# Routing one-hots written for eight of 32 rows, a later sum of the result, and 35 instead of 33 steps of y per phase

## The chip, the cores and the metric

The kernel runs on one core of one Trainium2 chip. The metric is the time of one execution on the device in microseconds (us); the median of three runs stands for a kernel. The profile is one more execution, recorded by the hardware profiler. Its engines are PE (TensorE, matmuls), PEld (its weight loads), DVE (VectorE), ACT (ScalarE), POOL (GpSimd) and SP (SyncE, which here only issues DMAs).

## The reference, cut to what matters

Attention (4 batches, 8 heads, 576 positions) gives 2304 tokens of 512 numbers, a dense layer pair makes `x` of them (2304 x 512), and a routed layer follows. Only the end of the dense pair (`y = g @ w_out`) and the routing are touched here:

```python
cap = N // E                      # 2304 // 8 = 288
logits = x @ w_gate
flat = logits.flatten()
order = np.argsort(-flat)
assigned = -np.ones(N); counts = np.zeros(E)
for idx in order:
    tok, e = idx // E, idx % E
    if assigned[tok] >= 0 or counts[e] >= cap:
        continue
    assigned[tok] = e
    counts[e] += 1
for e in range(E):
    mask = assigned == e
    out[mask] = np.maximum(x[mask] @ w1[e], 0.0) @ w2[e]
```

## The kernel before, in words

The kernel runs in stages: attention, the first dense product (`mlp_in`), then the second dense product y together with the routing, then the eight experts. This change lies in the stage of y and routing, from 592.7 to 846.3 us of the profiled span.

**y.** `MlpOut.run` (L1027) is a generator. It computes y for 18 tiles of 128 tokens, in 16 steps each, 288 steps in all. A step is three matmuls of 128x512 (L1038). After every fourth step `parts` has ACT copy the high parts of four blocks for the next tile, and POOL subtract them from the source to get the low parts (helper `split`, L497 and L502, one instruction of 128x512 on each). So POOL gets one such instruction for every four steps. When tile 16 is done, `ready` is set; `first.gather` then has POOL fetch the rows of the first expert's tokens from DRAM, while PE computes tile 17.

**Routing.** `routing` (L750) is a generator too. The greedy loop of the reference is done in seven phases; in each, one expert fills up. All 2304 tokens lie as 128 partitions x 18 columns (T = 18), with eight experts beside (NE = 8). In one phase:

- `best` (L795) finds for each token its best expert among those still open: a one-hot `bst`, and its key in two halves, `khi` and `klo`. Its last instruction, in `above` (L824), makes `G`, the comparison of the key with 40 thresholds (128x720, bf16).
- `oh` (L843) is `bst` times `U`, the tokens that are still free (128x144). `ohb` (L845) is its cast to bf16 in sixteen copies (128x2304), so that a count comes out on all 128 rows.
- Six rounds follow, three for each half of the key. A round is a `count` (L831): 18 small matmuls with the columns of `ohb` as weights and those of `G` as data. DVE reads the count (`sat`, L861), moves it across rows (`tq`, L863; `tb`, L868) and makes the next `G`.
- A last count (L889) with `GE` picks the expert that fills up. Then come `star`, `lim`, a prefix sum by two small matmuls (L911, L912), `best` of the next phase, and `U`.
- `final` (L834) adds the tokens that got a place to `FIN`: `ao` (L836) and the sum (L837). It stands behind the first count of the next phase.

**What sets the order.** All instructions are issued in the order in which the program is written, and each engine works through its own list in that order. In `build`, the loop `for t in routing(...)` takes a number from each `yield` of routing and issues that many steps of y before it goes on. The numbers are in the tuple YS:

```python
YS = (2, 9, 3, 4, 5, 4, 18, 3)
```

So on PE a phase is: 9 steps of y, first count, 3 steps, count, 3 steps, count, 4 steps, count, 3 steps, count, 3 steps, count, 3 steps, the count with `GE`, 5 steps, the prefix sum. That is 33 steps. PE can do y while DVE works on the routing, and it stands still where the steps in between are done before DVE is. Behind the seventh phase come 4 steps, the prefix sum over `FB` (L945), 18 steps, and the product that gives the permutation (L976); what is left of y follows.

Of the kernel before, what the change touches and what calls it, by code (L numbers as in the profile page):

```python
# [12 lines left out]
BF = mybir.dt.bfloat16  # L13
I32 = mybir.dt.int32
AF = mybir.ActivationFunctionType
OP = mybir.AluOpType
# [8 lines left out]
NE = 8  # L25
# [715 lines left out]
def bc(ap, axis, n):  # L741

    ap = ap.unsqueeze(axis)
    shape = list(ap.shape)
    shape[axis] = n
    return ap.to_broadcast(shape)
# [7 lines left out]
def routing(net, cst, pools, lg, perm, first, spare):  # L754
# [3 lines left out]
    tc, nc, io = net.tc, net.nc, net.io  # L758
    V = nc.vector
    rp, rw, rps = pools  # L760
    T = NTT

    def small(shape, name, dt=F32, **kw):
        return rw.tile(shape, dt, name=name, **kw)

    yield YS[0]
    L = rp.tile([128, T, NE], F32, name="L")
# [10 lines left out]
    U = rp.tile([128, T], F32, name="U")  # L778
    V.memset(U, 1.0)
    FIN = rp.tile([128, T, NE], F32, name="FIN")  # L780
# [5 lines left out]
    V.memset(remc, float(CAP))  # L786
    zs = rp.tile([128, T + 1], F32, name="zs")
    V.memset(zs[:, 0:1], 0.0)
    zero = rp.tile([128, 1], F32, name="zero")
    V.memset(zero, 0.0)  # L790
    wr = cst["eix"][:, 1]
# [30 lines left out]
    def above(key, base, rnd):  # L822
        G = small([128, T, 40], "G", BF)
        V.scalar_tensor_tensor(G, bc(key, 2, 40), base, bc(cst["thr"][:, rnd], 1, T),  # L824
                               op0=OP.subtract, op1=OP.is_ge)
        return G

    def count(G, ohb, n):
        cnt = rps.tile([128, n], F32, name="rps")
        for t in range(T):  # L830
            nc.tensor.matmul(cnt, ohb[:, t].rearrange("p a e -> p (a e)"), G[:, t], start=t == 0, stop=t == T - 1)  # L831
        return cnt

    def final(oh, A):  # L834
        ao = small([128, T, NE], "ao")
        V.tensor_tensor(out=ao, in0=oh, in1=bc(A, 2, NE), op=OP.mult)  # L836
        V.tensor_tensor(out=FIN, in0=FIN, in1=ao, op=OP.add)  # L837

    bst, khi, klo, G = best()
    last = None  # L840
    for ph in range(NE - 1):
        oh = small([128, T, NE], "oh", bufs=2)
        V.tensor_tensor(out=oh, in0=bst, in1=bc(U, 2, NE), op=OP.mult)  # L843
        ohb = small([128, T, 16, NE], "ohb", BF)
        V.tensor_copy(ohb, bc(oh, 2, 16))  # L845
        yield YS[1]

        key = khi
        for half in range(2):
            base = zero  # L850
            low = zero
            for rnd in range(3):
                cnt = count(G, ohb, 40)
                if rnd == half == 0 and last is not None:
                    final(*last)
                if rnd == 1:
                    low = small([128, 1], "low")
                    V.tensor_scalar(low, mx, 41.0, None, op0=OP.mult)
                sat = small([128, 40], "sat")
                num = small([128, 1], "num")  # L860
                V.tensor_scalar(sat, cnt, remc, 0.0, op0=OP.is_ge, op1=OP.add, accum_out=num)  # L861
                tq = small([128, 32], "tq")
                V.transpose(tq, num.to_broadcast([128, 32]))  # L863

                tb = small([128, 32], "tb")
                old = (zero, low, base)[rnd]
                base = small([128, 1], f"base{half}{rnd}")
                V.tensor_tensor_reduce(out=tb, in0=tq, in1=old.to_broadcast([128, 32]), op0=OP.add, op1=OP.max,  # L868
                                       scale=(1681.0, 41.0, 1.0)[rnd], scalar=0.0, accum_out=base)
                if rnd < 2:  # L870
                    G = above(key, base, rnd + 1)
                elif half == 0:
                    k2 = small([128, T], "k2")
                    V.tensor_scalar(k2, khi, base, 65536.0, op0=OP.subtract, op1=OP.mult)
                    V.tensor_tensor(out=k2, in0=k2, in1=klo, op=OP.add)
                    key = k2
                    G = above(key, zero, 0)
                else:
                    GE = small([128, 2, T], "GE", BF)
                    V.tensor_scalar(GE[:, 0], key, base, None, op0=OP.is_gt)  # L880
                    V.tensor_scalar(GE[:, 1], key, base, None, op0=OP.is_equal)
                if rnd == 0:
                    mx = small([128, 1], "mx")
                    V.tensor_reduce(out=mx, in_=tq, axis=mybir.AxisListType.X, op=OP.max)
                yield YS[2] if rnd < 2 else YS[3] if half == 0 else YS[7]

# [21 lines left out]
        V.tensor_copy(Zb, Z)  # L908
        yield YS[4]
        zp = rps.tile([128, 2, T], F32, name="rps")  # L910
# [12 lines left out]
        if ph < NE - 2:  # L923
            bst, khi, klo, G = best()
# [4 lines left out]
        A = small([128, T], "A")  # L929
        V.tensor_tensor(out=A, in0=GE[:, 0], in1=sel, op=OP.add)  # L930

        V.scalar_tensor_tensor(U, A, 0.0, U, op0=OP.is_equal, op1=OP.mult)
        last = oh, A
    final(*last)

    op = small([128, NE], "op")
    V.tensor_scalar(op, lim, 0.0, None, op0=OP.is_gt)
    V.tensor_copy(oh, bc(U, 2, NE))
    V.tensor_tensor(out=oh, in0=oh, in1=bc(op, 1, T), op=OP.mult)
    V.tensor_tensor(out=FIN, in0=FIN, in1=oh, op=OP.add)  # L940
    FB = small([128, T, NE], "FB", BF)
    V.tensor_copy(FB, FIN)
    yield YS[5]
    ps = rps.tile([128, 2, T, NE], F32, name="rps")
# [20 lines left out]
    V.tensor_tensor(out=ohk, in0=ge[:, :, 0:24], in1=ge[:, :, 1:25], op=OP.subtract)  # L965
    V.tensor_scalar(kx, kx, -96.0, 96.0, op0=OP.mult, op1=OP.add)
    V.tensor_tensor(out=kx, in0=kx, in1=slot, op=OP.add)
    ohq = small([128, T, 16, NE], "ohb", BF).rearrange("p t a e -> p t (a e)")[:, :, 0:96]
    V.tensor_tensor(out=ohq, in0=bc(kx, 2, 96), in1=bc(cst["q96"], 1, T), op=OP.is_equal)
    dig = small([128, T, 2, 24], "dig", BF)  # L970
    for d in range(2):
        V.tensor_tensor(out=dig[:, :, d], in0=ohk, in1=bc(cst["ids"][:, d], 2, 24), op=OP.mult)
    yield YS[6]
    ps = rps.tile([96, 2, 24], F32, name="rps")
# [13 lines left out]

YS = (2, 9, 3, 4, 5, 4, 18, 3)


class MlpOut:
# [369 lines left out]
```

## Time and profile before

| what | value |
|---|---|
| median of 3 runs | 1085.62 us (1083.53 to 1089.73) |
| the profiled execution | 1086.05 us, of which the span from the first to the last instruction is 1084.3 us |
| busy share of the span | PE 95%, PEld 74%, DVE 65%, ACT 44%, POOL 31% |
| granted TensorE clock, mean | 0.986 of full speed |
| chain that ended last, by engine | PE 60%, issue 18%, DVE 14%, POOL 4%, DMA 2%, ACT 1% |
| in it, lines of the routing | `rps` L831 2%, `G` L824 2%, `ohb` L845 1% |

The chain that ended last is followed back from the last instruction: at each step to what released it. A row of the timeline gives the start, the duration, the engine, the line, what is written and read, how often, and in brackets the idle time of the engine before it and what ended it. A matmul's row lasts longer than the time until the next one can start, since matmuls are pipelined.

### The profile page before, as it was taken

What the parts mean: (1) busy time and instruction counts of PE and PEld (TensorE: products, weight loads), DVE (VectorE), ACT (ScalarE), POOL (GpSimd) and SP (SyncE); (2) the same over time, 40 slices, a digit from 0 to 9 for tenths busy, and PEclk for the clock granted to TensorE, in tenths of its full rate; (3) what the DMA queues carried; (4) which work ended last, traced back from release to release, by engine and by line L of the source; (5) the groups of instructions that cost most, each with busy time, mean ns of one, the idle gap of its engine ahead of it and who ended that gap; (6) DMA issues with size and microseconds to landing.
All of it is one profiled execution on the core that took longest, in us unless ns stands there. A gap on an engine that the chain in (4) does not pass through costs nothing.

```text
span 1084.3 us, 20220 instructions
## 1 busy us (share of the span) xinstructions
PE 1029.3 (95%) x7815; PEld 804.1 (74%) x7815; DVE 700.6 (65%) x1734; ACT 480.3 (44%) x1034; POOL 336.4 (31%) x360
## 2 busy tenths in 40 slices
PE   8599999999999999999999899899999999999996
PEld 5255776666665777787776677677778899999996
DVE  7699566656667298864346788778874555555551
ACT  5477676766666232332225121121223455555552
POOL 1122333334334044322116444333434222222111
PEclk8899999999999999999999999999999999999998
DMA  5733332121200355643410262222212676555300
GB/s 131 178 95 98 102 94 69 35 70 34 86 1 2 89 204 191 214 146 127 148 57 6 64 233 79 78 71 87 64 56 89 221 255 199 200 194 194 112 24 22
DMA packets 75748, 119.76 MB, mean 110 GB/s; under 512 B 10340, under 2 KB 38272, under 8 KB 74116
## 3 DMA queue, kind: packets, MB, share of 16 engines
q1 hardware_dynamic: 70156, 104.81, 30.5%
q0 software_dynamic: 3136, 9.46, 2.8%
q10 hardware_dynamic: 2360, 4.20, 1.1%
q8 instruction: 61, 1.00, 0.4%
q14 instruction: 35, 0.29, 0.1%
HBM read 84.24 MB, written 23.60 MB: 99 GB/s over the span
## 4 chain that ended last, share of the span: by engine, by line
PE 60%; issue 18%; DVE 14%; POOL 4%; DMA 2%; ACT 1%; SPq 0%; POOLq 0%; DVEq 0%; ACTq 0%
PE hps L595 17%; PE yps L1038 10%; PE tr L289 8%; PE sc L232 8%; PE av L316 7%; PE sc L149 4%; POOL ye L1155 2%; POOL out_dram L1195 2%; PE rps L831 2%; DVE gall L134 2%; DVE G L824 2%; PE lacc L670 1%; DMA xh<-gall 1%; DVE P L244 1%; DVE ohb L845 1%
## 5 line engine op out<-in xcount | busy, mean ns | idle before, releaser
L261 POOL TENSOR_SCALAR P<-P,r 128x576 f32<-128x576 f32 x144 | 108.2, 763 | 234.9 <-DVE r L259 175.6
L595 PE MATMUL hps<-xh 128*128 128x512 f32 (+1 forms) x640 | 149.9, 376 | 1.2 <-DVE xh L502 1.2
L252 ACT ACTIVATE P<-P,nm 128x576 f32<-128x576 f32 x144 | 111.1, 772 | 64.0 <-DVE nm L244 61.3
L595 PEld LDWEIGHTS hps<-xh 128*128 128x128 f32 x640 | 110.8, 189 | 28.8 <-issue 7.3
L1038 PE MATMUL yps<-xh,g 128*128 128x512 f32 x336 | 117.0, 408 | 0.0
L232 PE MATMUL sc<-k,q 64*128 64x288 f32 (+1 forms) x640 | 104.0, 426 | 1.0 <-ACT PT L159 0.9
L289 PEld LDWEIGHTS tr<-ident,P 128*128 128x128 f32 x736 | 79.2, 141 | 30.4 <-issue 24.3
L289 PE MATMUL tr<-ident,P 128*128 128x128 f32 x736 | 97.8, 278 | 0.0
L316 PE MATMUL av<-PT,v 128*64 128x128 f32 (+3 forms) x880 | 95.4, 350 | 2.3 <-issue 1.4
L602 DVE TENSOR_TENSOR gall<-hps,sg 128x512 f32<-128x512 f32 (+1 forms) x77 | 48.1, 631 | 72.8 <-ACT sg L601 72.7
L1174 PE MATMUL mps<-xh 128*128 128x288 f32 x288 | 87.2, 303 | 0.8 <-DVE xl L1211 0.8
L1174 PE MATMUL mps<-xh,xl 128*128 128x288 f32 x288 | 85.0, 295 | 0.0
L1174 PE MATMUL mps<-xl,xh 128*128 128x288 f32 x288 | 84.9, 295 | 0.0
L316 PEld LDWEIGHTS av<-PT,v 128*64 128x64 f32 x880 | 49.1, 136 | 45.7 <-issue 23.5
L1038 PE MATMUL yps<-xh 128*128 128x512 f32 x240 | 81.9, 399 | 0.9 <-DVE wo L708 0.9
L601 ACT ACTIVATE sg<-hps 128x512 f32<-128x512 f32 (+1 forms) x77 | 42.4, 552 | 89.4 <-PE hps L595 86.4
L502 DVE TENSOR_TENSOR xl<-wo,xh 128x512 fp32r<-128x512 f32 (+1 forms) x56 | 51.4, 940 | 45.1 <-ACT xh L497 43.9
L1195 POOL DMA_INDIRECT out_dram<-o,perm x24 | 27.7, 1153 | 170.5 <-ACT o L1193 167.0
L595 PE MATMUL hps<-xl,xh 128*128 128x512 f32 (+1 forms) x320 | 79.4, 370 | 0.0
L265 ACT ACTIVATE PT<-tr 128x384 f32<-128x384 f32 (+2 forms) x176 | 73.3, 424 | 9.1 <-PE tr L289 8.5
L232 PEld LDWEIGHTS sc<-k,q 64*128 64x128 f32 (+1 forms) x640 | 55.5, 175 | 27.1 <-issue 10.9
L1038 PEld LDWEIGHTS yps<-xh,g 128*128 128x128 f32 x336 | 63.9, 190 | 13.8
(244 smaller groups left out, 2186.4 us busy)
## 6 DMA issues: line engine op xcount, KB each, us to landing
gd<-gall SPq DMA_DIRECT2D x12, 1152.0 KB
woraw<-in_moe_w_out_dram SPq DMA_DIRECT2D x16, 512.0 KB
wo<-in_moe_w_dram SPq DMA_DIRECT2D x4, 2048.0 KB
gall<-in_moe_w_dram SPq DMA_DIRECT2D x8, 1024.0 KB
wiraw<-in_moe_w_in_dram SPq DMA_DIRECT2D x14, 512.0 KB
xl<-gd SPq DMA_DIRECT2D x18, 384.0 KB
wiraw<-gd SPq DMA_DIRECT2D x18, 384.0 KB
wo<-in_moe_w_dram SPq DMA_DIRECT2D x6, 1024.0 KB
```

Of the source, the lines that this page charges most:

```text
L232: nc.tensor.matmul(out[:, hf, 0:288], q[rows, icol], k[rows, js[hf]], start=True, stop=True)
L252: nc.scalar.activation(Ps[hh], Ps[hh], AF.Exp, bias=nms[hh], scale=-1.0, accum_out=sums[:, hh:hh + 1])
L261: nc.gpsimd.tensor_scalar(p, p, r[:, hh:hh + 1], 1.0, op0=OP.mult, op1=OP.mult)
L265: nc.scalar.activation(out, in_, AF.Copy)
L289: nc.tensor.transpose(tr[:, k], P[:, c0:c0 + 128], ident)
L316: nc.tensor.matmul(ps[rows, :n], v[:, hh, jt], pt[:, 5 * hh + jt if jt < 4 else 4], start=jt == 0, stop=jt == NIT - 1)
L502: lo_eng.tensor_sub(lo, src, f(hi))
L595: nc.tensor.matmul(ps[:, :n], w[:, c], x[:, c, ts], start=k == 0, stop=k == len(seq) - 1)
L602: nc.vector.tensor_tensor(out=self.gall[:, ft % NG, t0:t0 + n], in0=ps[:, :n], in1=sg[:, :n], op=OP.mult)
L1038: nc.tensor.matmul(ps, g[:, ft % 4], w(ft), start=k == 0, stop=k == 47)
L1174: nc.tensor.matmul(ps, w[:, c], x[:, c], start=k == 0, stop=k == len(seq) - 1)
L1195: st = nc.gpsimd.indirect_dma_start(out=io["out"], out_offset=bass.IndirectOffsetOnAxis(ap=perm[:, 3 * e + r:3 * e + r + 1], axis=0), in_= ...
```

## The change

The change has four parts.

1. `ohb` becomes one tile of 18 x 4 x 32 columns that is zeroed once, by POOL. In each phase DVE writes eight of each 32 columns, straight from `bst` and `U`, as bf16 (128x576). A count so comes out on eight of each 32 rows, and zero on the others.
2. `oh` is now a bf16 copy (128x144) taken out of `ohb`, made behind it.
3. `final` becomes a generator: the product `ao` is issued in the second round of the first half, the sum in the second round of the second half, each behind the `G` for the third round.
4. YS[1] is 11 instead of 9, so a phase has 35 steps of y. Up to the end of routing 14 more steps are issued (269 of 288 instead of 255).

The last lines reuse other tiles (`rest` for `oh`, `ohb` for a new tile of the same name).

```diff
--- before.py
+++ after.py
@@ -786,6 +786,9 @@
     V.memset(remc, float(CAP))
     zs = rp.tile([128, T + 1], F32, name="zs")
     V.memset(zs[:, 0:1], 0.0)
+
+    ohb = rp.tile([128, T, 4, 32], BF, name="ohb")
+    nc.gpsimd.memset(ohb, 0.0)
     zero = rp.tile([128, 1], F32, name="zero")
     V.memset(zero, 0.0)
     wr = cst["eix"][:, 1]
@@ -832,17 +835,19 @@
         return cnt
 
     def final(oh, A):
+
         ao = small([128, T, NE], "ao")
         V.tensor_tensor(out=ao, in0=oh, in1=bc(A, 2, NE), op=OP.mult)
+        yield
         V.tensor_tensor(out=FIN, in0=FIN, in1=ao, op=OP.add)
+        yield
 
     bst, khi, klo, G = best()
-    last = None
+    last = iter(())
     for ph in range(NE - 1):
-        oh = small([128, T, NE], "oh", bufs=2)
-        V.tensor_tensor(out=oh, in0=bst, in1=bc(U, 2, NE), op=OP.mult)
-        ohb = small([128, T, 16, NE], "ohb", BF)
-        V.tensor_copy(ohb, bc(oh, 2, 16))
+        V.tensor_tensor(out=ohb[:, :, :, 0:NE], in0=bc(bst, 2, 4), in1=bc(bc(U, 2, 4), 3, NE), op=OP.mult)
+        oh = small([128, T, NE], "oh", BF, bufs=2)
+        V.tensor_copy(oh, ohb[:, :, 0, 0:NE])
         yield YS[1]
 
         key = khi
@@ -851,8 +856,6 @@
             low = zero
             for rnd in range(3):
                 cnt = count(G, ohb, 40)
-                if rnd == half == 0 and last is not None:
-                    final(*last)
                 if rnd == 1:
                     low = small([128, 1], "low")
                     V.tensor_scalar(low, mx, 41.0, None, op0=OP.mult)
@@ -869,6 +872,8 @@
                                        scale=(1681.0, 41.0, 1.0)[rnd], scalar=0.0, accum_out=base)
                 if rnd < 2:
                     G = above(key, base, rnd + 1)
+                    if rnd:
+                        next(last, None)
                 elif half == 0:
                     k2 = small([128, T], "k2")
                     V.tensor_scalar(k2, khi, base, 65536.0, op0=OP.subtract, op1=OP.mult)
@@ -930,14 +935,16 @@
         V.tensor_tensor(out=A, in0=GE[:, 0], in1=sel, op=OP.add)
 
         V.scalar_tensor_tensor(U, A, 0.0, U, op0=OP.is_equal, op1=OP.mult)
-        last = oh, A
-    final(*last)
+        last = final(oh, A)
+    for _ in last:
+        pass
 
     op = small([128, NE], "op")
     V.tensor_scalar(op, lim, 0.0, None, op0=OP.is_gt)
-    V.tensor_copy(oh, bc(U, 2, NE))
-    V.tensor_tensor(out=oh, in0=oh, in1=bc(op, 1, T), op=OP.mult)
-    V.tensor_tensor(out=FIN, in0=FIN, in1=oh, op=OP.add)
+    rest = small([128, T, NE], "ao")
+    V.tensor_copy(rest, bc(U, 2, NE))
+    V.tensor_tensor(out=rest, in0=rest, in1=bc(op, 1, T), op=OP.mult)
+    V.tensor_tensor(out=FIN, in0=FIN, in1=rest, op=OP.add)
     FB = small([128, T, NE], "FB", BF)
     V.tensor_copy(FB, FIN)
     yield YS[5]
@@ -965,7 +972,7 @@
     V.tensor_tensor(out=ohk, in0=ge[:, :, 0:24], in1=ge[:, :, 1:25], op=OP.subtract)
     V.tensor_scalar(kx, kx, -96.0, 96.0, op0=OP.mult, op1=OP.add)
     V.tensor_tensor(out=kx, in0=kx, in1=slot, op=OP.add)
-    ohq = small([128, T, 16, NE], "ohb", BF).rearrange("p t a e -> p t (a e)")[:, :, 0:96]
+    ohq = ohb.rearrange("p t a e -> p t (a e)")[:, :, 0:96]
     V.tensor_tensor(out=ohq, in0=bc(kx, 2, 96), in1=bc(cst["q96"], 1, T), op=OP.is_equal)
     dig = small([128, T, 2, 24], "dig", BF)
     for d in range(2):
@@ -988,7 +995,7 @@
 
 
 
-YS = (2, 9, 3, 4, 5, 4, 18, 3)
+YS = (2, 11, 3, 4, 5, 4, 18, 3)
 
 
 class MlpOut:
```

On DVE, around the first count of the second phase. The kernel before (the names are those of the text above; `rps` is the count):

```order
L932 SCALAR_TENSOR_TENSOR U<-A,U 128x18
L843 TENSOR_TENSOR oh<-bst,U 128x144
L845 CAST ohb<-oh 128x2304
L836 TENSOR_TENSOR ao<-oh,A 128x144
L837 TENSOR_TENSOR FIN<-FIN,ao 128x144
L861 TENSOR_SCALAR sat,num<-rps,remc 128x40
```

The changed kernel at the same place:

```order
L937 SCALAR_TENSOR_TENSOR U<-A,U 128x18
L848 TENSOR_TENSOR ohb<-bst,U 128x72x8
L850 COPY oh<-ohb 128x144
L864 TENSOR_SCALAR sat,num<-rps,remc 128x40
```

The first count on PE waits for `ohb`: one instruction stands between `U` and the count now, where there were two, and `ao` and `FIN` no longer stand ahead of `sat`.

On DVE, in the second and third round of the first half of that phase, the changed kernel has:

```order
L871 ISA base_6706 128x1
L827 SCALAR_TENSOR_TENSOR G<-khi,base_6706,thr 128x720
L840 TENSOR_TENSOR ao<-oh,A 128x144
L864 TENSOR_SCALAR sat,num<-rps,remc 128x40
L866 STREAM_TRANSPOSE tq<-num 128x32
```

The product `ao` now stands between the `G` of the third round and the `sat` that reads the third count; the sum `FIN` stands at the same place of the second half.

On POOL, where the stage of y begins, the changed kernel has (the rows at L502 are the low parts for y):

```order
L502 TENSOR_TENSOR g_6092<-gall,g_6091 128x512
L791 MEMSET ohb 128x2304
L502 TENSOR_TENSOR g_6094<-wiraw,g_6093 128x512
L502 TENSOR_TENSOR xh<-wiraw,xh 128x512 x2
```

The zeroing of `ohb` stands between the low parts for tile 0 and those for tile 1.

## Rows read from the trace of the kernel before

**Rows 1.** Busy time by stretch, stage of y and routing: start:end length, then each engine (instructions)
```profile
592.70:846.30 253.60, 234.87 (x1787) 184.24 (x1788) 189.21 (x616) 55.79 (x92) 102.01 (x75) 0.99 0.31 96
```
**Rows 2.** Waits of PE, 590 to 850 us: total us, times, longest
```profile
PE rps L831 <- DVE ohb L845: 13.1, 7, 3.1
PE rps L831 <- DVE G L824: 4.0, 9, 0.6
```
**Rows 3.** Timeline of PE at the first count of each phase
```profile
604.28 0.39 PE L831 MATMUL rps<-G,ohb 128*128 128x40 bf16 x9 [3.14 <-DVE ohb L845]
...
633.68 0.47 PE L831 MATMUL rps<-G,ohb 128*128 128x40 bf16 x12 [1.54 <-DVE ohb L845]
...
662.66 0.49 PE L831 MATMUL rps<-G,ohb 128*128 128x40 bf16 x13 [1.16 <-DVE ohb L845]
...
694.40 0.37 PE L831 MATMUL rps<-G,ohb 128*128 128x40 bf16 x8 [2.72 <-DVE ohb L845]
...
725.83 0.34 PE L831 MATMUL rps<-G,ohb 128*128 128x40 bf16 x7 [2.04 <-DVE ohb L845]
...
754.89 0.47 PE L831 MATMUL rps<-G,ohb 128*128 128x40 bf16 x12 [1.43 <-DVE ohb L845]
...
783.99 0.37 PE L831 MATMUL rps<-G,ohb 128*128 128x40 bf16 x8 [1.08 <-DVE ohb L845]
```
**Rows 4.** Timeline of PE at the second count of phases two and seven
```profile
636.99 0.28 PE L831 MATMUL rps<-G,ohb 128*128 128x40 bf16 x5 [0.53 <-DVE G L824]
...
787.29 0.28 PE L831 MATMUL rps<-G,ohb 128*128 128x40 bf16 x5 [0.49 <-DVE G L824]
```
**Rows 5.** Timeline of PE at the sixth count of phase one
```profile
618.89 0.28 PE L831 MATMUL rps<-G,ohb 128*128 128x40 bf16 x5 [0.37 <-DVE G L824]
```
**Rows 6.** Groups of DVE, 590 to 850 us: count, busy us, mean ns, idle before
```profile
L845 DVE CAST ohb<-oh 128x2304 bf16<-128x2304 f32 x7 | 9.5, 1360 | 0.2
...
L824 DVE SCALAR_TENSOR_TENSOR G<-khi,zero,thr 128x720 bf16<-128x720 f32 x7 | 6.8, 968 | 0.0
L836 DVE TENSOR_TENSOR ao<-oh,A 128x144 f32<-128x144 f32 x7 | 6.5, 922 | 0.0
...
L843 DVE TENSOR_TENSOR oh<-bst,U 128x144 f32<-128x144 f32 x7 | 2.2, 307 | 0.2
```
**Rows 7.** Timeline of DVE behind the last phase: products with two inputs
```profile
812.74 0.63 DVE L961 TENSOR_TENSOR wiraw<-slot,k 128x450 f32<-128x450 f32 x1
...
815.53 3.10 DVE L969 TENSOR_TENSOR ohb<-kx,q 128x1728 bf16<-128x1728 f32 x1
```
**Rows 8.** Chain that ended last, in order of time: steps of y in the stage
```profile
604.90 2.19 PE yps L1038 x9
...
695.04 3.72 PE yps L1038 x9
...
810.06 12.51 PE yps L1038 x54
```
**Rows 9.** Busy time by stretch behind the fourth stall; the clock is third from the end
```profile
694.00:698.00 4.00, 3.60 (x25) 2.94 (x26) 2.76 (x11) 0.18 (x1) 0.00 (x0) 0.61 0.00 0
```
**Rows 10.** Timeline of DVE and POOL at the first count of phase three
```profile
658.59 1.82 POOL L502 TENSOR_TENSOR g<-wiraw,g 128x512 fp32r<-128x512 f32 x1 [1.65 <-ACT g L497]
661.39 2.36 POOL L502 TENSOR_TENSOR g<-gall,g 128x512 fp32r<-128x512 f32 x1 [0.98 <-ACT g L497]
...
661.25 1.36 DVE L845 CAST ohb<-oh 128x2304 bf16<-128x2304 f32 x1
662.52 1.39 DVE L836 TENSOR_TENSOR ao<-oh,A 128x144 f32<-128x144 f32 x1
```
**Rows 11.** Groups of POOL: a fill of 128x144 and the low parts, mean ns
```profile
L502 POOL TENSOR_TENSOR xh<-wiraw,xh 128x512 fp32r<-128x512 f32 x11 | 14.5, 1318 | 16.4 <-ACT xh L497 13.9 <-PE rps L889 2.4
...
L730 POOL MEMSET rst<- 128x144 f32 x1 | 0.2, 220 | 0.0
```
**Rows 12.** Timeline at the end of y: last matmuls, store of tile 16, first gather
```profile
845.89 0.39 PE L1038 MATMUL yps<-xh 128*128 128x512 f32 x1
...
835.88 0.33 SPq L1054 DMA_DIRECT2D yd<-y  x1
...
839.04 1.04 POOL L1118 DMA_INDIRECT xl<-yd,perm  x1 [4.76 <-DVE xl L502]
...
846.12 0.58 PE L1128 MATMUL xps<-ident,xl 96*128 96x96 f32 x4
```

## The prediction

> **What bounds the kernel now.** I read the waits of PE first, then the timeline around each, then the groups of DVE. In the stage of y and routing (253.60 us) PE is busy for 234.87 us, DVE for 189.21, POOL for 102.01 [rows 1]. PE has the most work, and what it does is fixed, so the stage gets shorter only where PE stands still. The waits say where that is: 13.1 us in seven stalls for `ohb` and 4.0 us in nine stalls for `G` [rows 2]. The seven are one per phase, at the first count, 3.14, 1.54, 1.16, 2.72, 2.04, 1.43 and 1.08 us [rows 3]. There the nine steps of y are done and DVE is still on its way from the count with `GE` over `best`, `U` and `oh` to `ohb`. So here DVE's chain sets the time, and each microsecond taken from it, or covered by another step of y, is a microsecond of the kernel.
>
> The stalls aren't scattered. Count the steps of y that have been issued when the count with `GE` starts, from which the chain runs: 30, 63, 96, 129, 162, 195 for phases two to seven. Modulo four that is 2, 3, 0, 1, 2, 3, and the stalls are 1.54, 1.16, 2.72, 2.04, 1.43, 1.08 [rows 3]: equal remainders give stalls equal within 0.11 us. POOL gets one low part per four steps, and it is what delays DVE. The clearest case is in phase three: POOL's instruction takes 2.36 us where the mean of its kind is 1.32, because the cast of `ohb` is running, and `ao` behind the cast takes 1.39 us where `oh`, of the same size, takes 0.31 [rows 6, 10, 11].
>
> **The change, part by part.**
>
> *The one-hots.* Removed from the chain: `oh`, 0.31, and the cast, 1.36 us [rows 6]. Added: one product of two inputs with 576 elements. The nearest rows are 0.63 us for 450 elements and 0.97 for 720 [rows 6, 7]; in between, 576 gives 0.63 + 126/270 x 0.34 = 0.79. The chain gets 0.31 + 1.36 - 0.79 = 0.88 us shorter. Bounds: not below 0.31, the product of 144; above, 0.79 and a hold by a whole low part of POOL, 1.32 [rows 11], so 2.1 us (the row of 1728 elements with a bf16 output, 3.10 us [rows 7], would be 1.03 for 576). I take 0.79, because the product at this very place, `oh`, was held in none of its seven phases: its mean is 0.307 [rows 6]. [...]
>
> *Two more steps of y ahead of the first count.* 54 matmuls take 12.51 us [rows 8], 0.232 each, so a step is 0.695 and two are 1.39 us. Together with the 0.88, each stall loses up to 2.27 us. But the remainders move too. The count with `GE` now starts after 32, 67, 102, 137, 172, 207 steps, remainders 0, 3, 2, 1, 0, 3. With the stall that each remainder had, less 2.27: phase two 0.45, three to five none, six 0.45, seven none. Phase one has another chain, 3.14 - 2.27 = 0.87. Left are 1.8 of 13.1, gain **11.3 us**.
>
> *The sum moved away.* `ao` (mean 0.92) and `FIN` stood between `ohb` and `sat`. In phases two, three, six and seven the second count then waited about half a microsecond for its `G`, 0.53 in the first and 0.49 in the last of these four [rows 4], and `ao` was held there as in rows 10. Now `sat` starts when the count is there. Gain 4 x 0.50 = **2.0 us**. In its new place, behind the `G` of the third round, `ao` or `FIN` runs while PE does three steps (2.09 us) and the count; it costs nothing as long as that cover holds. If POOL holds it, 1.08 us more (1.39 - 0.31), part of that is late at the third `sat`; I take nothing and keep this for a rival. The same goes for the copy `oh`: it is covered by the first count.
>
> *Restarts.* A matmul's row lasts 0.39 us and the next starts 0.23 after it [rows 12], so a stall in the profile is 0.16 us shorter than the time it costs. Four stalls for `ohb` and four for `G` go: 8 x 0.16 = **1.3 us**.
>
> *The clock.* [...] The longest stall left is below 1 us. Gain **1.5 us**.
>
> *New stalls for `G`.* Of nine, five are not of the kind above; together 4.0 - 2.0 = 2.0, 0.4 each, such as 0.37 in phase one [rows 2, 5]. Most stand in rounds that start at remainder zero. With 35 steps per phase seven rounds start so (one each). I count two more, 2 x (0.4 + 0.16) = **1.1 us lost**.
>
> *The fill by POOL.* 144 elements take 0.22 us [rows 11], 2304 at most sixteen times that, 3.5 us, once. It is issued after two steps. Behind it wait POOL's low parts for tile 1, which PE reaches at step 17, so 14 steps or 9.7 us later at the least. The first `ohb` on DVE waits for it too, at the end of a chain that reaches PE at 604.28 [rows 3], 11.6 us after the stage begins [rows 1]. Nothing.
>
> *The end of the stage.* 14 steps move ahead of the permutation; 19 are behind it instead of 33. The gather of the first expert's rows hangs on the store of tile 16: issued at 835.88, gather at 839.04, PE needs it at 846.12 [rows 12]. All three keep their distance to tile 16, whose last three steps now follow the permutation product. The permutation then has 2.1 us and the store's 3 us of cover. Nothing.
>
> Sum: 11.3 + 2.0 + 1.3 + 1.5 - 1.1 = 15.0 us. The profiled execution is 1086.05 us (span 1084.3 and 1.75 around it), 0.43 above the median of the runs. 1086.05 - 15.0 = **1071 us**.
>
> **The rivals.**
>
> *The write of `ohb` is held in each phase.* Then it costs 2.1 instead of 0.79, the chain is 0.43 longer than before, and each stall loses only 1.39 - 0.43 = 0.96. By remainder 2.18 + 1.76 + 0.20 + 0.5 + 1.08 + 1.76 + 0.12 = 7.6 us are left instead of 1.8: 1071 + 5.8 = 1076.8 us. For it: the cast never lost to POOL, the product may. Against it: `oh`'s mean above.
>
> *Slower: POOL's holds eat more than the gain.* Places: the seven writes of `ohb`, seven copies `oh`, six `ao`, six `FIN`; each can be held while a low part runs, 1.08 us as in rows 10, and the three steps of a round cover only the round's own chain. From 14 uncovered holds on (15.0/1.08) the kernel is slower; with all 26 it is 1071 + 28 = 1099 us. For it: POOL is busy for 40% of the stage [rows 1], and `ao`'s mean of 0.92 against 0.31 means four holds in seven [rows 6]. Against it: `ao` was held because the cast had kept POOL waiting and POOL was next in turn; without the cast that order is gone, and 40% of 26 is 10, most of them covered. [...]
>
> *No change: y's own supply becomes the bound.* If ACT, POOL and the loads can't follow a faster PE, the stalls return as waits of y: near 1086 us. Against it: one low part of 1.32 us per four steps of 0.695, less than half of POOL's time, and of PE's waits in this stretch, whose two longest are [rows 2], none is for POOL.
>
> *Better than forecast.* No stall left at `ohb` and no new one at `G`: 15.0 + 1.8 + 1.1 = 17.9, and about 1068 us; with most old `G` stalls gone too, 1067.
>
> **How the numbers follow.** A measurement of this kernel can tell about 0.5% from no change, 5.4 us. My forecast has 0.68, the held write 0.18, better than forecast 0.06, no change 0.05, slower 0.03. The first three are faster by over 0.5%: 0.92. The range goes from 1067 (the better case) to 1077.5 (the held write, and 0.7 for the scatter of runs).
>
> **What would show it.** In the profile of the changed kernel: `ohb` as a product of some 0.8 us; PE's waits for it near 2 us in all, in phases one, two and six; no wait at the second count behind `ao`; `ao` and `FIN` behind a `G`, without a wait at the third count; 9 matmuls after each first count at about 2.2 us; the gather some 3 us after the store of tile 16. The prediction is wrong if `ohb`'s mean is near 2 us, if waits for `G` grow beyond 6 us, or if PE waits at L1128 for the gather.

## The result and the profile after

The changed kernel takes 1073.91 us (median of 4 runs, 1072.77 to 1076.27), the kernel before 1084.61 on the same chip (4 runs, 1083.53 to 1089.73). The ratio, of the means, is 0.9895 [0.9874, 0.9916]: faster by 1.05%, twice the 0.5% that the prediction took as what a measurement can tell. The forecast was 1071.0 with a range of 1067 to 1077.5. The direction held and the time lies in the range, but the gain (of the medians) is 10.7 us where 15.0 were forecast.

First, where the 10.7 us are. Busy time by stretch of the changed kernel, from the first matmul of y to the first matmul that takes the gathered rows (start:end, length, busy us of PE, weight loads, DVE, ACT, POOL with instructions, granted clock, DMA share, GB/s):

```profile
591.12:833.80 242.68, 233.46 (x1786) 183.65 (x1786) 188.25 (x616) 55.81 (x92) 104.62 (x76) 0.99 0.32 100
```

Between the same two instructions the kernel before took 253.37 us (592.75 to 846.12). 253.37 - 242.68 = 10.7 us, the whole difference of the medians. PE executes the same 1786 matmuls, and is busy for about a microsecond less; the rest is idle time that has gone. The spans of the two profiled executions differ by more, 1084.3 - 1070.6 = 13.7 us: 1.6 us lie ahead of this stage and 1.4 behind it. The code there is the same, and these parts differ by as much among the runs below (the stage starts between 590.59 and 592.97 us), so they aren't counted as part of the change.

The waits of PE in the changed kernel, 590 to 850 us, total, times, longest (before: [rows 2]):

```profile
PE rps L834 <- DVE G L827: 4.1, 9, 0.7
PE rps L834 <- DVE ohb L848: 3.7, 2, 3.2
PE rps L952 <- DVE FB L949: 1.3, 1, 1.3
```

Seven stalls for `ohb` have become two, 13.1 us have become 3.7. The stalls for `G` are as many as before and as long, though not the same ones. The timeline of PE at the first counts that still stall, phases one and two (before: [rows 3]):

```profile
604.15 0.72 PE L834 MATMUL rps<-G,ohb 128*128 128x40 bf16 x18 [3.23 <-DVE ohb L848]
...
636.16 0.62 PE L834 MATMUL rps<-G,ohb 128*128 128x40 bf16 x18 [0.47 <-DVE ohb L848]
```

Phase two stalls for 0.47 us (0.45 forecast), phases three to seven not at all. Phase one is as it was: 3.23 us, 3.14 before. So nearly everything that is left stands in one place. The groups of DVE, 590 to 850 us (count, busy us, mean ns, idle before; before: [rows 6]):

```profile
L848 DVE TENSOR_TENSOR ohb<-bst,U 128x576 bf16<-128x576 f32 x7 | 5.3, 757 | 0.2
...
L850 DVE COPY oh<-ohb 128x144 bf16<-128x144 bf16 x7 | 4.3, 616 | 0.2
L842 DVE TENSOR_TENSOR FIN<-FIN,ao 128x144 f32<-128x144 f32 x7 | 4.2, 601 | 0.0
...
L840 DVE TENSOR_TENSOR ao<-oh,A 128x144 f32<-128x144 bf16 x7 | 3.2, 459 | 0.0
```

The product takes 0.757 us, and was held in no phase. The copy `oh` and the two parts of the sum are held at times (0.616 us on average for a copy that takes 0.20 when nothing holds it), behind cover, as forecast.

Then the clock. The chain that ended last, in order of time, behind the first count of phase one (before: [rows 8]):

```profile
604.87 3.58 PE yps L1045 x9
```

And the busy time of this stretch, the clock third from the end (before, at phase four: [rows 9]):

```profile
604.00:608.00 4.00, 3.85 (x26) 3.20 (x27) 2.19 (x10) 0.00 (x0) 0.00 (x0) 0.57 0.02 4
```

The nine slow matmuls have moved from phase four (3.72 us) to phase one (3.58), where they took 2.19 before. The granted clock is 0.57 over these 4 us, and 0.50 from 605 to 607 us; in the kernel before it is 1.00 from 604 to 608 us.

Why does phase one still stall? POOL there (timeline of the changed kernel):

```profile
595.16 2.01 POOL L791 MEMSET ohb<- 128x2304 bf16 x1
597.13 1.30 POOL L502 TENSOR_TENSOR g<-wiraw,g 128x512 fp32r<-128x512 f32 x1
598.39 2.55 POOL L502 TENSOR_TENSOR xh<-wiraw,xh 128x512 fp32r<-128x512 f32 x2
600.91 1.25 POOL L502 TENSOR_TENSOR g<-gall,g 128x512 fp32r<-128x512 f32 x1
```

And DVE beside it:

```profile
595.75 0.31 DVE L805 TENSOR_TENSOR eq<-Lm,m 128x144 f32<-128x144 f32 x1
595.98 1.23 DVE L808 TENSOR_SCALAR sg<-m 128x18 int32<-128x18 int32 x1
...
598.61 1.12 DVE L815 TENSOR_SCALAR hi_i<-sg 128x18 int32<-128x18 int32 x1
599.65 1.34 DVE L816 TENSOR_SCALAR lo_i<-sg 128x18 int32<-128x18 int32 x1
600.90 1.44 DVE L818 TENSOR_TENSOR bst<-eq,em 128x144 f32<-128x144 f32 x1
...
602.46 0.97 DVE L827 SCALAR_TENSOR_TENSOR G<-khi,zero,thr 128x720 bf16<-128x720 f32 x1
603.34 0.75 DVE L848 TENSOR_TENSOR ohb<-bst,U 128x576 bf16<-128x576 f32 x1
```

POOL never rests between 593.9 and 602.2 us. Its fill of `ohb` takes 2.01 us, the low parts behind it come one right after the other, and each of DVE's small instructions ends about when one of POOL's does: 1.12, 1.34 and 1.44 us for what took 0.16, 0.16 and 0.30 in the kernel before. The fill itself holds one, `sg` (1.23 us, ending with the fill; 0.17 where nothing holds it), but not the `eq` of two inputs just ahead of it. From this comes the theory tested below, **theory A**: each stall here is a chain of DVE that is too long for PE's cover, and what makes it too long is POOL, whose fill and low parts hold DVE's instructions. The rivals in the expectations each put one of the terms elsewhere.

### The profile page after: what moved, and what is told of

It is laid out like the page before. It is cut to its first block, busy times and chain, and to the rows that moved or that the text cites. A ratio compares the mean times of both kernels' runs of the same rounds, so it can differ in the third digit from the quotient of the medians.

```text
span 1070.6 us, 20215 instructions
## 1 busy us (share of the span) xinstructions
PE 1029.0 (96%) x7815; PEld 803.8 (75%) x7815; DVE 700.0 (65%) x1734; ACT 480.4 (45%) x1034; POOL 339.4 (32%) x361
## 4 chain that ended last, share of the span: by engine, by line
PE 65%; issue 18%; DVE 9%; POOL 4%; DMA 2%; ACT 1%; SPq 0%; POOLq 0%; DVEq 0%; ACTq 0%
PE hps L595 18%; PE yps L1045 15%; PE tr L289 8%; PE sc L232 8%; PE av L316 7%; PE sc L149 4%; POOL ye L1162 2%; PE rps L834 2%; POOL out_dram L1202 2%; DVE gall L134 2%; DVE G L827 1%; PE lacc L670 1%; DVE P L244 1%; DMA xh<-gall 1%; DMA woraw<-in_moe_w_out_dram 1%
## 5 line engine op out<-in xcount | busy, mean ns | idle before, releaser
L502 DVE TENSOR_TENSOR xl<-wo,xh 128x512 fp32r<-128x512 f32 (+1 forms) x56 | 51.4, 941 | 36.7 <-ACT xh L497 36.7
L1045 PEld LDWEIGHTS yps<-xh,g 128*128 128x128 f32 x336 | 63.7, 190 | 13.7
```

The source lines that it names most:

```text
L502: lo_eng.tensor_sub(lo, src, f(hi))
L1045: nc.tensor.matmul(ps, g[:, ft % 4], w(ft), start=k == 0, stop=k == 47)
```

## The experiments

The kernel before was run beside each group on the same chip; a ratio is to that. "Before" and "changed" in the edits say which kernel was edited. The first seven runs take the change apart, the rest go for the two causes of what is left.

### The fill given to ACT

```diff
  (changed)
-    nc.gpsimd.memset(ohb, 0.0)
     V.memset(zero, 0.0)
+    nc.scalar.activation(ohb.rearrange("p t a e -> p (t a e)"), zero.to_broadcast([128, T * 128]), AF.Copy)
```

> The changed kernel, with the zeroes of ohb written by ACT instead of POOL. Theory A (the fill of 2.01 us on POOL pushes the low parts behind it onto the first chain of DVE): the stall for ohb in phase one falls from 3.23 us to about 0.9, what was forecast for it, the matmuls behind it stay at full clock (nine in 2.2 us, not 3.58), and the time falls by 2.3 to 3.8 us from the changed kernel's 1073.9, to about 1070.5. Theory B (POOL's low parts for tiles 0 and 1 hold that chain whether the fill is there or not): the stall stays near 3 us and the time near 1074.

1070.56 us, ratio 0.9864 [0.9849, 0.9879]. PE at the first count of phase one, timeline:

```profile
601.58 0.62 PE L834 MATMUL rps<-G,ohb 128*128 128x40 bf16 x18 [1.19 <-DVE ohb L848]
```

The chain that ended last, behind it:

```profile
602.20 2.21 PE yps L1045 x9
```

POOL and DVE in front of it, timeline:

```profile
596.34 1.40 POOL L502 TENSOR_TENSOR g<-wiraw,g 128x512 fp32r<-128x512 f32 x1 [1.66 <-ACT g L497]
597.70 3.20 POOL L502 TENSOR_TENSOR xh<-wiraw,xh 128x512 fp32r<-128x512 f32 x2
600.87 1.79 POOL L502 TENSOR_TENSOR g<-gall,g 128x512 fp32r<-128x512 f32 x1
...
596.12 0.17 DVE L815 TENSOR_SCALAR hi_i<-sg 128x18 int32<-128x18 int32 x1
...
596.27 0.30 DVE L818 TENSOR_TENSOR bst<-eq,em 128x144 f32<-128x144 f32 x1
...
599.69 1.83 DVE L848 TENSOR_TENSOR ohb<-bst,U 128x576 bf16<-128x576 f32 x1
```

Without the fill on POOL the stall is 2.04 us shorter, as long as the fill was, and the nine matmuls are back at 2.21 us: 2.04 + 1.37 = 3.4 us by the trace, and the ratio differs from the changed kernel's by 0.0031, which is 3.4 us of 1086 (two chips, and the intervals just overlap). DVE's small instructions are at 0.17 and 0.30 again. The product is held here in phase one, 1.83 us, while POOL's low parts run. The edit does a second thing: ACT's fill puts off ACT's copies, so POOL stands still for 1.66 us ahead of its low parts, and DVE's small instructions run in that gap. The next run changes POOL's fill alone.

### Half the fill

```diff
  (changed)
-    nc.gpsimd.memset(ohb, 0.0)
+    nc.gpsimd.memset(ohb.rearrange("p t a e -> p (t a e)").bitcast(F32), 0.0)
```

> The changed kernel, with POOL writing the zeroes of ohb as 1152 words instead of 2304 half words. Theory A (what counts in phase one is how long POOL is taken): a fill of about 1.0 us instead of 2.01, a stall in phase one between e1's 1.19 and the changed kernel's 3.23, near 2.2, and a time 1 to 2.5 us below the changed kernel's. Theory B (only whether POOL is behind, not by how much): the stall stays near 3.2 and the time where it was.

1071.82 us, ratio 0.9883 [0.9868, 0.9898]; the changed kernel on this chip has 1073.54 and 0.9896 [0.9879, 0.9912], so the times alone don't tell them apart. POOL's fill, and PE at the first count of phase one, timelines:

```profile
596.56 1.07 POOL L791 MEMSET ohb<- 128x1152 f32 x1
...
604.54 0.62 PE L834 MATMUL rps<-G,ohb 128*128 128x40 bf16 x18 [2.23 <-DVE ohb L848]
```

A fill of 2.01, 1.07 and no us on POOL makes a stall of 3.23, 2.23 and 1.19: about one for one. The product is held once here too (1.82 us), and the nine matmuls behind the stall take 2.19. So the fill's time lies on the path, which the forecast had ruled out.

### Two more steps alone

```diff
  (before)
-YS = (2, 9, 3, 4, 5, 4, 18, 3)
+YS = (2, 11, 3, 4, 5, 4, 18, 3)
```

> The kernel before with 11 steps of y ahead of the first count and nothing else. Theory A (each step covers 0.695 us of DVE's chain): the stalls for ohb fall by 1.39 us each where there is so much, by remainder to 1.75, 1.33, 0, 0.15, 0.65, 1.33 and 0, 5.2 us instead of 13.1, and the time falls by 8 to 9.5 us to about 1076. Theory B (the 14 steps taken from behind the permutation are missed there, and PE waits for the gather): a wait of PE at L1128 of several us, and a time near that of before, 1084.

1076.12 us, ratio 0.9921 [0.9907, 0.9935]. Three stalls for `ohb` are left, in phases one, two and four: 2.81, 1.41 and 0.42 us, 4.6 in all where 5.2 were expected. The time came as expected, the places only in part. Phase two (1.33) is right, phase four has 0.42 for 0.15, phases five and six have none for 0.65 and 1.33, and phase one has 2.81 where 3.14 - 1.39 = 1.75 were due. Waits for `G` rise from 4.0 us in nine to 6.0 in eleven. Timelines of POOL and DVE in phase one:

```profile
600.44 1.31 POOL L502 TENSOR_TENSOR g<-gall,g 128x512 fp32r<-128x512 f32 x1 [1.51 <-ACT g L497]
...
600.55 1.37 DVE L843 TENSOR_TENSOR oh<-bst,U 128x144 f32<-128x144 f32 x1
```

There is no fill in this kernel. Two more steps also let one more low part through, at step 12, and it falls on `oh`: 1.37 us for 0.31, 1.06 more. A step of y as cover brings its share of POOL's work with it. In the forecast a step was only PE's time.

### The change without the steps

```diff
  (changed)
-YS = (2, 11, 3, 4, 5, 4, 18, 3)
+YS = (2, 9, 3, 4, 5, 4, 18, 3)
```

> The changed kernel with 9 steps instead of 11. Theory A (the chain is shorter by 0.88 us in each phase, and the count behind the old place of the sum is free): stalls for ohb of about 4.6 (3.23 and two steps), 0.66, 0.28, 1.84, 1.16, 0.55 and 0.20, 9.3 us in all, no wait at the second count, a time of about 1079. Theory B (the narrow write isn't worth anything, as POOL holds it where it never held the cast): stalls as before, 13 us, and a time of 1082 to 1084.

1076.89 us, ratio 0.9925 [0.9909, 0.9942]. Waits of PE, 590 to 850 us:

```profile
PE rps L834 <- DVE ohb L848: 7.7, 7, 3.4
PE rps L834 <- DVE G L827: 2.5, 7, 0.6
```

The stalls for `ohb` in phases two to seven are 0.57, 0.20, 1.77, 1.09, 0.49 and 0.17 us. Taken from [rows 3], that is 0.97, 0.96, 0.95, 0.95, 0.94 and 0.91 less: the shorter chain is worth the same in each phase, 0.95 on average where 0.88 was forecast. Phase one has 3.43 (4.6 expected); less 0.88 it would be 2.26, so the fill costs 1.17 there, without the steps. With the low part of step 12, which cost 1.06 in the run before, that is 2.23, and the changed kernel has 2.36 more than forecast (3.23 against 0.87). The gains of this run and of the one before don't add up to that of the changed kernel (0.75% and 0.79% against 1.05%): much of each stall is taken away by either.

### The sum alone

```diff
  (before)
-                if rnd == half == 0 and last is not None:
-                    final(*last)
...
                     G = above(key, base, rnd + 1)
+                    if rnd:
+                        next(last, None)
```

> The kernel before with the sum alone moved behind the second round of each half; cast and 9 steps as before. Theory A: the four stalls of half a microsecond at the second counts of phases two, three, six and seven go, waits for G fall from 4.0 to 2.0 us, and the time by 2 to 2.6 us to about 1082. Theory B (the sum is only held in its new place instead): as much appears at the third counts, and the time stays at 1084.6.

1083.58 us, ratio 0.9978 [0.9966, 0.9989], 2.4 us. Waits of PE, 590 to 850 us:

```profile
PE rps L831 <- DVE ohb L847: 13.1, 7, 3.1
PE rps L831 <- DVE G L824: 2.4, 5, 0.7
```

Four stalls for `G` and 1.6 us go; with four restarts of 0.16 that is 2.2, by the forecast 2.0 and 0.6. This term held, by the waits and the times. In the profiled execution the stage is only 0.45 us shorter (252.92 against 253.37): behind the stall of 2.04 us in phase five nine matmuls take 3.49 us there, and 2.15 in the profiled execution of the kernel before.

### One product of all sixteen copies

```diff
  (before)
-        V.tensor_copy(ohb, bc(oh, 2, 16))
+        V.tensor_tensor(out=ohb, in0=bc(bst, 2, 16), in1=bc(bc(U, 2, 16), 3, NE), op=OP.mult)
```

> The kernel before, with all sixteen copies written by one product of two inputs (128x2304) from bst and U instead of a cast of oh; 9 steps and the sum as before. [...] Theory B (one instruction instead of two is what counts): about 1.4 us for it, stalls of 11 us, and 1082.

1100.88 us in one run. The group of DVE that holds the product:

```profile
L845 DVE TENSOR_TENSOR ohb<-bst,U 128x2304 bf16<-128x2304 f32 x7 | 17.9, 2551 | 0.0
```

The waits of PE, 590 to 850 us:

```profile
PE rps L831 <- DVE ohb L845: 20.4, 7, 4.0
```

So it is the size that makes the product worth it: with 2304 elements it takes 2.55 us, 1.19 more than the cast (1.11 ns an element, where the cast takes 0.59), and with 576 0.757. `oh` is still computed ahead of it in this kernel, so there are two instructions as before, and theory B, that their number counts, isn't tested. The stalls are 20.4 us where the kernel before has 13.1 [rows 2], and the time is 12.65 us above its 1088.23 on this chip. A part of that shows in the chain that ended last, the nine matmuls behind the first count (of four phases):

```profile
604.58 4.02 PE yps L1038 x9
...
637.18 3.41 PE yps L1038 x9
...
...
701.82 3.50 PE yps L1038 x9
734.30 3.06 PE yps L1038 x9
```

They are slow in all seven phases, 3.06 to 4.02 us; over 2.19 us each that is 9.4 us in all. Here every stall, from 2.16 to 3.96 us, was followed by slow matmuls; the granted clock was 0.59 and 0.60 over the 4 us at the first counts of phases two and three.

### No low parts from the third tile on

```diff
  (changed)
-        split(nc, nc.scalar, nc.gpsimd, hi, lo, src)
+        if tt < 2:
+            split(nc, nc.scalar, nc.gpsimd, hi, lo, src)
+        else:
+            nc.scalar.activation(hi, src, AF.Copy)
```

> The changed kernel, but POOL doesn't write the low parts of y's blocks from tile 2 on: y is then computed with old low parts, and the routing decides on the same logits as before. Theory A (the stalls for G are DVE instructions that wait for POOL's low parts): from phase two on no wait of PE for G or ohb is left, where the changed kernel has six for G (2.5 us) and one for ohb (0.47 us); copies, products and casts on DVE all take their short times (ao and FIN 0.31, oh copy 0.20, tb 0.19). Theory B (the rounds' three steps are too short by themselves): waits of 0.2 us or more stay in most rounds.

1068.97 us in one run. Of all waits at the counts one is left (timeline of PE, phase one, where POOL's work is as in the changed kernel):

```profile
605.87 0.62 PE L834 MATMUL rps<-G,ohb 128*128 128x40 bf16 x18 [3.21 <-DVE ohb L848]
```

No stall for `G` is left, none for `FB`. In the groups of DVE `ao` is at 301 ns on average and the copy `oh` at 199, the times of instructions that nothing holds. So POOL's low parts make all nine stalls for `G`.

### The changed kernel again, and spare steps

The changed kernel on a third chip:

> The changed kernel as it is, beside the next three on one chip: near 0.9895 of the kernel before.

1073.54 us, ratio 0.9896 [0.9879, 0.9912], with the stalls as above: 3.7 us for `ohb` in two, 3.6 for `G` in nine.

Then, with the fill on ACT, two more steps ahead of the first count of phase one and one behind the last phase:

```diff
  (the fill on ACT)
-        yield YS[1]
+        yield YS[1] + (0 if ph else 2)
...
-YS = (2, 11, 3, 4, 5, 4, 18, 3)
+YS = (2, 11, 3, 4, 5, 5, 18, 3)
```

> The kernel of e1 with the three steps that are left to place before tile 16 ends: two more ahead of the first count of phase one, one more ahead of the product over FB. Theory A (steps of y cover DVE's chain wherever PE waits): the stall of 1.19 us in phase one goes, the one of 1.24 us for FB falls to about 0.55, and the time falls by 1.5 to 2 us from e1's 1070.6, to about 1069. Theory B (what is covered in one place comes back in another, since all later phases now start two steps later against POOL's low parts): the same time within 1 us, with stalls for ohb in phase four, whose count with GE then starts at remainder zero.

1068.24 us, ratio 0.9816 [0.9801, 0.9832]. No wait for `ohb` is left; 2.3 us for `G` in seven, 0.9 for `FB` (0.55 expected). On the third chip:

> The kernel of e5 again, on this chip: 0.9816 of the kernel before within its interval, 5 to 6 us below the changed kernel.

1066.49 us, ratio 0.9833 [0.9819, 0.9846], with the same waits; 7.0 us below the changed kernel there.

### Aligned phases: a miss, and a hit

In the changed kernel a round of three steps stalls for `G` when a low part starts in the middle of DVE's chain: the eight rounds that start at a multiple of four steps all do, by 0.17 to 0.70 us (one of them has four steps). Phases of 36 steps, a multiple of four, should then show the same picture in each phase. First with the low parts also asked for two steps earlier within their four:

```diff
  (the fill on ACT)
-                if ft % 4 == 3:
+                if ft % 4 == 1:
...
-                yield YS[2] if rnd < 2 else YS[3] if half == 0 else YS[7]
+                yield YS[2] if rnd < 2 else YS[3] - (ph == NE - 2) if half == 0 else YS[7]
...
-YS = (2, 11, 3, 4, 5, 4, 18, 3)
+YS = (2, 11, 3, 5, 5, 4, 18, 3)
```

> The kernel of e1 with phases of 36 steps, so that each phase stands at the same place against POOL's low parts: five steps ahead of the fourth count (four in the last phase), and the low parts issued two steps earlier, so that the first count of each phase starts three steps behind one. 275 steps up to the permutation, three more than tile 16 has. Theory A (a round of three steps stalls if and only if it starts as a low part is due, and with this order only the last round, which has more cover, does): waits for G fall from 4.2 to below 1 us, no wait for ohb from phase two on, and the time falls by 3 to 4.5 us from e1's 1070.6, less up to 1 us by which the gather may come late, to about 1067. Theory B (the wait moves with the low part to another round): 4 us of waits for G stay, and the time is 1070 or, with the late gather, 1072.

1071.59 us, ratio 0.9848 [0.9829, 0.9866], with 5.4 us for `G` in 13 stalls: a miss. Timeline of PE, POOL and DVE at a count with 124 steps issued, a multiple of four:

```profile
695.24 0.62 PE L834 MATMUL rps<-G,ohb 128*128 128x40 bf16 x18
...
695.97 1.29 POOL L502 TENSOR_TENSOR xh<-gall,xh 128x512 fp32r<-128x512 f32 x1 [2.04 <-ACT xh L497]
...
696.45 0.86 DVE L871 CUSTOM_DVE_ANT_0 tb<-tq,low 128x32 f32<-128x32 f32 x1
...
698.37 0.61 PE L834 MATMUL rps<-G,ohb 128*128 128x40 bf16 x18 [0.37 <-DVE G L827]
```

The low part starts 0.73 us behind the count, as it does at 124 steps in the changed kernel. It waits for ACT's copy, which waits 2.70 us for a matmul of y, and not for its place in the program: issuing it earlier doesn't move it. Aligned phases with the low parts at the wrong place repeat the stall in every phase. Here the product is held in three phases, too: 1.89, 1.74 and 1.83 us, 1.21 on average. So, with the low parts as they were, the rounds themselves were moved, by two steps in phase one:

```diff
  (the fill on ACT)
-        yield YS[1]
+        yield YS[1] + (0 if ph else 2)
...
-                yield YS[2] if rnd < 2 else YS[3] if half == 0 else YS[7]
+                yield YS[2] if rnd < 2 else YS[3] - (ph == NE - 2) if half == 0 else YS[7]
...
-YS = (2, 11, 3, 4, 5, 4, 18, 3)
+YS = (2, 11, 3, 5, 5, 4, 18, 3)
```

> As e10, but with the low parts issued where the changed kernel has them, and the alignment made by two more steps in phase one instead, so that every first count starts after a number of steps that leaves three when divided by four. 277 steps up to the permutation. In e10 the low parts had stayed where they were against the count of steps, and rounds stalled where a low part began 0.6 to 1.4 us behind their count. Theory A (a low part comes at every fourth step whatever is done to its issue, so the number of steps alone decides): from phase two on the only round whose count is followed by a low part at that distance is the one behind the sixth count, which has 0.5 us more cover; waits for G fall below 1.5 us in all, no wait for ohb, and the time is 1 us below e5's if the gather isn't late, up to 1.5 us above it if it is. Theory B: more than 3 us of waits for G.

1065.32 us, ratio 0.9818 [0.9805, 0.9832]. Waits of PE, 590 to 850 us:

```profile
PE rps L952 <- DVE FB L949: 1.2, 1, 1.2
...
PE rps L834 <- DVE G L827: 0.9, 3, 0.3
```

Nothing is left at `ohb`, and 0.9 us at `G`. The 36 steps per phase also bring PE to the gathered rows early: its weight loads wait for them, 0.23 and 0.17 us. This is the fastest of the kernels, 8.2 us below the changed one on the same chip (1073.54); that it beats the version with spare steps (1066.49 there) isn't shown, since the two intervals overlap.

## Why the prediction was right, and what it missed

| Term | forecast, us | measured, us |
|---|---|---|
| stalls for `ohb` | 11.3 | 13.1 - 3.7 = 9.4 |
| stalls for `G`, moved sum and new ones | 4.0 - 2.8 = 1.2 | 4.0 - 4.1 = -0.1 |
| restarts, net | 1.3 - 0.3 = 1.0 | 5 x 0.16 = 0.8 |
| clock | 1.5 | 3.72 - 3.58 = 0.1 |
| sum | 15.0 | 10.2 (stage 10.7) |

The 1.5 us for the clock are 3.72 - 2.19 of [rows 8], and the changed kernel's run doesn't show them as a gain: nine matmuls take 3.58 us in phase one instead. With the fill on ACT they take 2.21.

**What held.** The chain from the count with `GE` to `ohb` was the bound: each phase gained what it lost in length, and two steps covered the rest. The price of the product (0.79; 0.757) held, and so did the remainders for the `ohb` stalls in phases two to five and seven; phase six, forecast 0.45, has none. The sum alone gave 2.4 us. The stalls for `G` at remainder zero came as forecast, in eight rounds instead of seven (phase four has two such). The end of the stage cost nothing. The gather against the store of tile 16, timelines of SP, POOL and PE in the changed kernel:

```profile
823.57 0.33 SPq L1061 DMA_DIRECT2D yd<-y  x1
...
826.72 1.04 POOL L1125 DMA_INDIRECT xl<-yd,perm  x1 [5.63 <-issue]
...
833.80 1.45 PE L1135 MATMUL xps<-ident,xl 96*128 96x96 f32 x9
```

3.15 us from the store to the gather, 3.16 before [rows 12], and PE waits for nothing there.

**What held by luck.** That the product was held nowhere belongs to the places of these 35-step phases against the low parts, and not to the product: in the aligned kernel that missed it was held in three of seven phases. The rule of the remainders was read from phases of 33 steps, which move by one step per phase against the 16 steps of a tile, so the one phase with remainder zero (96 steps) stood at the end of a tile. Phase two of the changed kernel (32 steps) does so too, phase six (172) doesn't. The low part behind the count with `GE`, at 623.75 us in phase two and at 741.06 in phase six (timeline of POOL):

```profile
625.14 1.31 POOL L502 TENSOR_TENSOR g<-wiraw,g 128x512 fp32r<-128x512 f32 x1 [2.72 <-ACT g L497]
...
741.78 1.29 POOL L502 TENSOR_TENSOR g<-gall,g 128x512 fp32r<-128x512 f32 x1 [2.06 <-ACT g L497]
```

In phase two ACT first copies the finished tile of y (0.60 us at 623.95), and the low part comes 1.39 us behind the count instead of 0.72. The two steps alone showed the same, 1.41 us in phase two and none in phase six. That the place in the tile decides is read from these rows; no run tests it by itself.

**What failed** is the step "The fill by POOL ... Nothing", in part the step on the two more steps, and with them phase one's "3.14 - 2.27 = 0.87". The fill itself was bounded well (2.01 us, at most 3.5 said). The cover was looked for in the wrong place: the prediction asked when PE needs POOL's low parts and when DVE needs the filled tile, and both are late enough. It didn't ask what a POOL that never rests does to DVE's instructions beside it, though its own slower rival had that mechanism and its price (1.08 us a hold). In phase one the stall was 3.23 us, 2.36 above the forecast: by the runs 1.17 for the fill and 1.06 for the low part of step 12, which the step "Two more steps of y" had left out, as it counted a step as PE's time alone. The nine matmuls then ran at the granted clock of 0.57 (over 4 us), behind a stall that should have been short: 3.58 - 2.19 = 1.39. Two stalls for `G`, 0.68 and 0.61, were also not counted in phase one; with the fill on ACT there are still nine stalls for `G` and 4.2 us, so they aren't the fill's. Together 2.36 + 1.39 + 1.29 = 5.0, less the 0.45 of phase six: 4.6, against the 4.3 missing (15.0 - 10.7). So nearly all that was mis-sized stands in phase one. The range held the time all the same, but its upper end (1077.5) was set by the held write, which didn't come; for what came the sum had no term.

The rivals: the held write did not come in the changed kernel (mean 757 ns; for the other runs see above), nor holds that eat the gain. The sums and copies are held, as the row of `FIN` (601 ns on average against 304 without low parts) shows, but behind PE's three steps. The holds go both ways: a low part of POOL beside the cast took 2.36 us [rows 10] where the mean is 1.32 [rows 11], and `tb` on DVE beside a low part of 1.29 took 1.20 in the changed kernel instead of 0.19. Without the low parts from the third tile on, the means are 301 ns for `ao`, 304 for `FIN`, 199 for the copy `oh` and 192 for `tb`. The fill, which only writes, held `sg` all the same (1.23 us instead of 0.17).

## What to carry to other kernels

An instruction that is moved to an idle-looking engine is not free because its result is needed late (the fill of 2.01 us on POOL made the stall 2.04 us longer than the fill on ACT did): ask which instructions of the other engines it will stand beside, and whether one of those ends a chain. Where work is interleaved as cover, a step brings all its instructions on all engines (here two more steps brought a low part that cost 1.06 us), so count how many of them fall into the chain that it is meant to cover. Where two rhythms meet (four steps to a low part, 35 to a phase), list the remainders before choosing the numbers; phases of 36 steps from the right start took the stalls for `G` from 4.2 us to 0.9.

## What the runs showed of the hardware

POOL's fill took its time by elements and not by bytes here: 2304 of bf16 2.01 us, and 1152 of f32, the same bytes, 1.07. ACT wrote the 2304 in 2.12 us, from one column.

Even DVE's smallest instructions were held for nearly the whole of one of POOL's, 1.29 us: 18 elements of int32 took 1.34 us instead of 0.17, rows of 32 took 1.20 instead of 0.19. The second of these in the timeline of POOL, DVE and PE, phase four of the changed kernel:

```profile
704.57 1.29 POOL L502 TENSOR_TENSOR xh<-wiraw,xh 128x512 fp32r<-128x512 f32 x1 [2.66 <-ACT xh L497]
704.70 1.20 DVE L871 CUSTOM_DVE_ANT_0 tb<-tq,zero 128x32 f32<-128x32 f32 x1
...
706.97 0.61 PE L834 MATMUL rps<-G,ohb 128*128 128x40 bf16 x18 [0.66 <-DVE G L827]
```

That one hold of 1.0 us becomes a stall of 0.66.

How fast PE goes on after a stall isn't given by the stall's length alone. Nine matmuls took 3.06 to 4.02 us instead of 2.2, with a granted clock of 0.57 to 0.61 over 4 us where it was read, after 2.72 us (before, phase four), after 2.81 (the two steps alone, phase one), after 3.21 to 3.43 (phase one of the changed kernel in both executions, without the steps and without the low parts) and after 2.16 to 3.96 (all seven with the wide product), and not after 3.14 (before, phase one), 2.23 (half the fill) or 1.19 (the fill on ACT). After 2.04 us in phase five they took 3.49 with the sum alone and 2.15 in the kernel before. What decides was not found; the slow matmuls cost 0.9 to 1.8 us each time, and no stall below 2 us was seen ahead of them.
